# Gated decode attention: keys and values of an item loaded together, x and gate as rows, the normaliser in the PSUM copy

## The chip, the cores and the metric

The kernel runs on one core of a Trainium2 chip. The metric is device time in microseconds (us) of one launch. Five engines run their own instruction lists: TensorE (PE, matmuls), VectorE (DVE), ScalarE (ACT), GpSimd (POOL) and SyncE (SP). Loads are issued by SP and ACT into DMA queues that 16 DMA engines work off.

## The reference

Two decode tokens (B = 2) attend over a cache of 4096 keys and values in 32 heads of 128; beside it stands a small feed-forward network, and a gate mixes both. All is float32.

```python
g = sigmoid((x * gate_w).sum(-1, keepdims=True))            # x: (2, 1, 640)
q = (x @ wq).reshape(B, 1, 32, 128).transpose(0, 2, 1, 3)
p = softmax(einsum("bhqd,bhkd->bhqk", q, k_cache) * 128**-0.5)
a = einsum("bhqk,bhkd->bhqd", p, v_cache).transpose(0, 2, 1, 3).reshape(B, 1, 4096) @ wo
b = silu(x @ w1) @ w2                                       # w1: (640, 1728)
out = g * a + (1 - g) * b
```

Keys and values are 134 MB each, so nearly all of the 298 MB read are cache.

## The kernel before

The 64 pairs of token and head are cut into 16 items: item i is one group of four heads (hq) for one token (b), the two tokens of a group one after the other. The keys of an item fill one slab of 128 partitions x 16384 floats (8.39 MB): 32 partitions a head, 128 keys on each. The values fill another. All large loads go through one pool of three slabs ("slots"), SLOTS = 3.

What is loaded when is a list written by hand, `stream`: first the query weights `wq` 0 and `wq` 1 (the second with w1), then key and value slabs, in the middle a slab `mid` (w2 and two groups of wo), at the end a slab `end` (six groups of wo). `pump` issues the next loads on SP in the order of the list, each as soon as the load three places earlier is spent; `spend` is called behind the last instruction that reads a slab. SP waits in order, so a load that has to wait holds back those behind it. The order of the instructions on each engine is that of the code (a manual schedule).

For an item, `scores` multiplies the key slab in place by the query (POOL takes the columns from CV on, VectorE the first CV = 88 of 128), VectorE sums over the head dimension, and the key slab is spent. `peak` finds the maximum of each 32 partitions, `weights` takes the exponentials on ACT with the sums beside them, `total` adds the sums with a matmul, `values` multiplies the weights with the value slab (32 matmuls into `pv`) and spends it, `combine` copies `pv` out of PSUM on ACT and picks the wanted blocks with four matmuls, and `scale` multiplies by the gate and the inverse of the total on VectorE. `permute` turns an output group with 16 small matmuls, and `project` multiplies it with wo into the accumulator `acc`, as `ffn_out` does with w2.

Ahead of the items stand `gates` (the sigmoid of the gate), `query_rows` (x @ wq), `query` (one group's query spread over the partitions) and `ffn_in` (x @ w1 and silu). x comes as `xs`, 128 partitions of 2 x 5 floats, and the gate as `gs`, 128 x 5, in runs of 20 bytes on ACT's queue. x is padded to 32 columns in `xz`, the stationary operand of all these matmuls.

Of the kernel before, what the change touches and what calls it, by code (L numbers as in the profile page):

```python
# [15 lines left out]
def tile_gated_decode(  # L16
# [66 lines left out]
    def load_wo(grp, t):  # L83
        at = WO_AT[grp][1]
        nc.sync.dma_start(  # L85
            t[:, at : at + Q * D],
            wo[grp * QD : (grp + 1) * QD, :].rearrange("(p n) d -> p (n d)", n=Q),
        )
# [62 lines left out]
    pz, rs = [], []  # L151
    for i in range(2):
        t = const.tile([P, NG, 32], F32, name=f"pz{i}")
        nc.gpsimd.memset(t, 0.0)
# [1 line left out]
        t = const.tile([P, Q], F32, name=f"rs{i}")
        nc.gpsimd.memset(t, 0.0)
        rs.append(t)
    o_first = const.tile([P, Q, 32], F32, name="o_first")
    nc.gpsimd.memset(o_first, 0.0)  # L160

    nc.vector.tensor_copy(xz[:, :, :B], xs.rearrange("p b j -> p j b"))  # L162
# [4 lines left out]
    def gates():
        gx = const.tile([P, B, J], F32, name="gx")
        nc.vector.tensor_mul(gx, xs, gs[:, None, :].to_broadcast([P, B, J]))  # L169
# [32 lines left out]
    def ffn_in():  # L202
        w = T["wq", 1][:, W1_AT : W1_AT + J * F].rearrange("p (j f) -> p j f", j=J)
        rows = ps_s.tile([P, 512], F32, tag="sm", name="hr")
        for j in range(J):
            for c in range(Q):
                nc.tensor.matmul(  # L207
                    rows[32 * c : 32 * c + 32, :QF],
                    xz[:, j, :],
                    w[:, j, c * QF : (c + 1) * QF],  # L210
                    start=(j == 0),
                    stop=(j == J - 1),
                )
        hrow = work.tile([P, 512], F32, tag="osb", name="hrow")
        nc.scalar.copy(hrow[:, :QF], rows[:, :QF])
        tail = ps_s.tile([P, 512], F32, tag="sm", name="hr")
        for j in range(J):
            nc.tensor.matmul(
                tail[:32, :FT], xz[:, j, :], w[:, j, FM:F], start=(j == 0), stop=(j == J - 1)
            )  # L220
        nc.scalar.copy(hrow[:32, QF : QF + FT], tail[:32, :FT])
# [1 line left out]
        ph = ps_s.tile([P, 512], F32, tag="sm", name="ph")
        for n in range(FR):
            for c in range(Q):
                q = slice(32 * c, 32 * c + 32)
                nc.tensor.matmul(  # L227
                    ph[q, n * B : (n + 1) * B],
                    hrow[q, n:QF:FR],
                    ident[q, 32 * c : 32 * c + B],  # L230
                    start=True,
                    stop=True,
                )
        nc.tensor.matmul(
            ph[:FT, FR * B : (FR + 1) * B], hrow[:32, QF : QF + FT], ident[:32, :B], start=True, stop=True
        )
        for n0, n1, m in ((0, FR, P), (FR, FR + 1, FT)):
            k = n1 - n0
            src = ph[:m, n0 * B : n1 * B].rearrange("p (n b) -> p n b", b=B)
            e = const.tile([P, k, B], F32, name=f"he{n0}")[:m]  # L240
            nc.scalar.activation(e, src, AF.Exp, scale=-1.0)  # L241
            nc.vector.tensor_scalar_add(e, e, 1.0)  # L242
# [46 lines left out]
    CV = 88  # L289
    S, M, R, PV, PO, O = {}, {}, {}, {}, {}, {}  # L290

    def scores(i):
# [9 lines left out]
        nc.vector.reduce_sum(S[i], k, axis=AX.X)  # L302
        spend("k", i)

    def peak(i):
        m = work.tile([P, 1], F32, name="m")
        nc.vector.reduce_max(m, S[i], axis=AX.X)  # L307
# [1 line left out]
        nc.vector.tensor_scalar_mul(mb, m.to_broadcast([P, 32]), -SCALE)  # L309
# [1 line left out]
        nc.vector.transpose(mt, mb)
# [34 lines left out]
    def combine(i):  # L346
        osb = work.tile([P, 4, DH], F32, tag="osb", name="osb")
        nc.scalar.copy(osb.rearrange("p c d -> p (c d)"), PV[i])  # L348
# [5 lines left out]
        PO[i] = po

    def scale(i):
        hq, b = items[i]
        r = work.tile([P, Q], F32, name="rinv")
        nc.vector.reciprocal(r, R[i][:, :Q])  # L359
        if b == 0:  # L360
            O[hq] = const.tile([P, Q, B], F32, name=f"oT{hq}")
        nc.vector.scalar_tensor_tensor(  # L362
            O[hq][:, :, b], PO[i][:, :Q], g[:, b : b + 1], r, op0=ALU.mult, op1=ALU.mult
        )

    OP = {}

    def permute(grp):  # L370
        pp = ps_s.tile([P, 512], F32, tag="sm", name="pp")
        for n in range(Q):
            for h in range(Q):
                nc.tensor.matmul(
                    pp[32 * h : 32 * h + 32, n * B : (n + 1) * B],
                    ident[:, n : P : Q],
                    O[grp][:, h, :],
                    start=True,
                    stop=True,
                )  # L380
        OP[grp] = o_first if grp == 0 else const.tile([P, Q, B], F32, name=f"oP{grp}")
        nc.scalar.copy(OP[grp][:, :, :B], pp[:, : Q * B].rearrange("p (n b) -> p n b", b=B))

# [20 lines left out]
    for i in range(N + 1):  # L404
        if i < N:
            scores(i)
            peak(i)
# [2 lines left out]
            weights(i)  # L410
        if i >= 1:
            total(i - 1)
            values(i - 1)
            combine(i - 1)
            scale(i - 1)
        if i == MID + 1:
            middle()
        if i > 2 * WO_MID and i % 2 == 0:
            permute(i // 2 - 1)
# [30 lines left out]
```

## Time and profile before

| | us |
|---|---|
| median of 3 runs | 723.04 (719.76 to 723.85) |
| the profiled execution's own time | 720.28 |
| its span | 718.5 |
| VectorE busy | 504.2 |
| PE busy | 225.8 |
| POOL busy | 179.4 |
| ACT busy | 48.7 |

The span is what the profiler sees of one execution; 1.78 us lie around it. A row of the timeline reads: start, duration, engine, line, operation, output<-input, and in brackets the idle time before it and what ended it. A row of a stretch reads: from:to and its length, busy time of PE, PE's weight load, VectorE, ACT and POOL with the number of instructions, the clock granted to PE, the busy share of the DMA engines and GB/s. A matmul in float32 shows as two records.

### The profile page before, as it was taken

The page shows a single profiled execution, that of the slowest core. Times are in us where ns is not written, and L with a number is a line of the kernel's source. Part 1 is how long each engine was busy: PE and PEld are TensorE (multiplying, and loading weights), DVE is VectorE, ACT ScalarE, POOL GpSimd, SP SyncE. Part 2 cuts the span into 40 slices and gives each one's busy share as a digit, 9 for nine tenths or more (in the row PEclk, how much of TensorE's full clock was granted, in tenths as well). Part 3 has the DMA queues.
Part 4 walks back from the last instruction along what each step waited for, and adds up shares of the span by engine and source line. Part 5 has one row for each costly group of instructions (what it writes and reads, how often), then busy time and mean ns, then how long its engine had stood idle before and what let it go on. Part 6 is the DMA issues. An engine that isn't in the chain of part 4 may idle for free.

```text
span 718.5 us, 4776 instructions
## 1 busy us (share of the span) xinstructions
PE 225.8 (31%) x2078; PEld 98.6 (14%) x2078; DVE 504.2 (70%) x153; ACT 48.7 (7%) x168; POOL 179.4 (25%) x28
## 2 busy tenths in 40 slices
PE   0081022141321406065051524225040615041474
PEld 0021000111110202024011121102010211011123
DVE  1007999797969595970786959595959778695920
ACT  0010010101010101010010010101010101001010
POOL 1006601404123150600606041321406060604100
PEclk9996557565565756577565656656575657565589
DMA  9999976899999999999999999999999999999995
GB/s 409 404 426 464 412 293 292 347 413 423 449 412 460 417 449 417 421 433 409 434 435 434 435 423 452 413 441 431 438 431 420 445 431 431 441 424 439 413 414 245
DMA packets 7013, 298.57 MB, mean 416 GB/s; under 512 B 1160, under 2 KB 1168, under 8 KB 1232
## 3 DMA queue, kind: packets, MB, share of 16 engines
q1 hardware_dynamic: 6568, 298.26, 96.6%
q8 instruction: 16, 0.26, 0.1%
q10 hardware_dynamic: 424, 0.01, 0.0%
q14 instruction: 5, 0.04, 0.0%
HBM read 298.26 MB, written 0.01 MB: 415 GB/s over the span
## 4 chain that ended last, share of the span: by engine, by line
DMA 52%; DVE 43%; PE 3%; issue 1%; ACT 0%; SPq 0%; DVEq 0%; ACTq 0%
DMA k<-in_A_k_cache_dram 43%; DVE s L302 24%; DVE k L298 17%; DMA gs<-in_gate_w_dram 5%; DMA end<-in_A_wo_dram 4%; DVE he L242 2%; PE qr L266 1%; DVE mb L309 1%; PE hr L207 1%; DVE m L307 0%; PE ph L227 0%; ACT pz L318 0%; PE po L351 0%; SPq L85 0%; PE acc L191 0%
## 5 line engine op out<-in xcount | busy, mean ns | idle before, releaser
L295 POOL TENSOR_TENSOR k<-k,qsb 128x5120 f32<-128x5120 f32 x16 | 176.5, 11034 | 486.9 <-DMA k<-in_A_k_cache_dram 486.9
L302 DVE TENSOR_REDUCE s<-k 128x128 f32<-128x16384 f32 x16 | 275.5, 17220 | 1.9
L337 PE MATMUL pv<-v,pz 128*32 128x512 f32 x1024 | 146.9, 738 | 300.6 <-DMA v<-in_A_v_cache_dram 300.6
L298 DVE TENSOR_TENSOR k<-k,q 128x11264 f32<-128x11264 f32 x16 | 190.2, 11886 | 62.2 <-DMA k<-in_A_k_cache_dram 62.2
L337 PEld LDWEIGHTS pv<-v,pz 128*32 128x32 f32 x1024 | 38.0, 133 | 396.3 <-issue 261.4
L318 ACT ACTIVATE pz<-s,nb 32x128 f32<-32x128 f32 x64 | 25.5, 398 | 551.1 <-DVE rinv L359 508.2
L362 DVE SCALAR_TENSOR_TENSOR oT<-po,g,rinv 128x4 f32<-128x4 f32 x16 | 3.6, 222 | 77.1 <-PE po L351 77.1
L351 PE MATMUL po<-sel,osb 128*128 128x4 f32 x128 | 27.0, 334 | 96.5 <-ACT osb L348 96.5
L351 PEld LDWEIGHTS po<-sel,osb 128*128 128x128 f32 x128 | 25.6, 296 | 111.0 <-ACT osb L348 111.0
L242 DVE TENSOR_SCALAR he<-he 128x26 f32<-128x26 f32 (+1 forms) x2 | 11.1, 5553 | 17.6 <-ACT he L241 17.6
L329 PE MATMUL tot<-rs,ones 128*128 128x4 f32 x32 | 8.1, 324 | 44.7 <-issue 44.7
L162 DVE COPY xz<-xs 128x10 f32<-128x10 f32 x1 | 0.2, 173 | 24.1 <-DMA xs<-in_A_x_dram 24.1
L329 PEld LDWEIGHTS tot<-rs,ones 128*128 128x128 f32 x32 | 8.4, 321 | 44.9 <-issue 44.9
L173 PE MATMUL gl<-gp,ones 128*128 128x2 f32 x2 | 0.6, 364 | 38.6 <-DVE gp L171 38.6
L318 ACT ACTIVATION_READ_ACCUMULATOR pz<-s,nb 32x1 f32 x64 | 11.8, 184 | 0.0
L266 PE MATMUL qr<-wq,xz 128*32 128x512 f32 x80 | 10.3, 674 | 0.0
L348 ACT COPY osb<-pv 128x512 f32<-128x512 f32 x16 | 9.4, 585 | 11.3 <-PE pv L337 11.0
L424 DVE COPY ot<-acc 128x160 f32<-128x160 f32 x1 | 0.3, 325 | 13.2 <-PE acc L191 13.2
L191 PE MATMUL acc<-end,oP 128*2 128x160 f32 x192 | 7.4, 299 | 5.1 <-DMA end<-in_A_wo_dram 5.1
L283 PE MATMUL q<-qrow,spread 128*128 128x128 f32 x32 | 8.2, 400 | 0.0
L169 DVE TENSOR_TENSOR gx<-xs,gs 128x10 f32<-128x10 f32 x1 | 0.2, 170 | 10.1 <-DMA gs<-in_gate_w_dram 10.1
L309 DVE TENSOR_SCALAR mb<-m 128x32 f32<-128x32 f32 x16 | 6.6, 410 | 0.6
(53 smaller groups left out, 80.3 us busy)
## 6 DMA issues: line engine op xcount, KB each, us to landing
v<-in_A_v_cache_dram SPq DMA_DIRECT2D x2, 4096.0 KB
end<-in_A_wo_dram SPq DMA_DIRECT2D x6, 1280.0 KB, 19.3
wq<-in_B_w_dram SPq DMA_DIRECT2D x1, 4320.0 KB, 36.7
mid<-in_B_w_dram SPq DMA_DIRECT2D x1, 4160.0 KB, 44.3
mid<-in_A_wo_dram SPq DMA_DIRECT2D x2, 1280.0 KB, 32.7
wq<-in_A_wq_dram SPq DMA_DIRECT2D x1, 2048.0 KB, 26.8
k<-in_A_k_cache_dram SPq DMA_DIRECT2D x16, 47.6
v<-in_A_v_cache_dram SPq DMA_DIRECT2D x15, 28.7
```

The costliest lines, as they stand in the source:

```text
L242: nc.vector.tensor_scalar_add(e, e, 1.0)
L266: nc.tensor.matmul(ps[u][32 * q : 32 * q + 32, :], xz[:, j, :], w[:, u * half : (u + 1) * half, q, :], start=(j == 0), stop=(j == J - 1),)
L283: nc.tensor.matmul(qps[hq][:, b, :], spread[:, b, :], qrow[:, hq, :], start=True, stop=True)
L295: nc.gpsimd.tensor_mul(k[:, CV:, :], k[:, CV:, :], qsb[hq][:, b, None, :].to_broadcast([P, C - CV, DH]))
L298: nc.vector.tensor_mul(k[:, :CV, :], k[:, :CV, :], qps[hq][:, b, None, :].to_broadcast([P, CV, DH]))
L302: nc.vector.reduce_sum(S[i], k, axis=AX.X)
L309: nc.vector.tensor_scalar_mul(mb, m.to_broadcast([P, 32]), -SCALE)
L318: nc.scalar.activation(pz[i % 2][lo:hi, :, 4 * q : 4 * q + 4], S[i][lo:hi].rearrange("p (g c) -> p g c", c=4), AF.Exp, bias=M[i][lo:hi], s ...
L329: nc.tensor.matmul(t[:, :Q], ones, rs[i % 2], start=True, stop=True)
L337: nc.tensor.matmul(PV[i][32 * q : 32 * q + 32, :], pz[i % 2][:, gr, :], v[:, gr, :], start=(gr < 4), stop=(gr >= NG - 4),)
L348: nc.scalar.copy(osb.rearrange("p c d -> p (c d)"), PV[i])
L351: nc.tensor.matmul(po[:, :Q], osb[:, c, :], sel[:, c : 4 * Q : 4], start=(c == 0), stop=(c == 3))
```

## The change

- **Order of the loads.** Up to item 5 keys and values of an item follow each other (k0, v0, k1, v1, ...), then come k6, `mid`, k7, v6, k8, v7 and so on. Before, the keys stood one item ahead throughout. The last group of wo is loaded in two pieces.
- **x and gate as rows.** They are loaded as two and one rows of 640 floats into spare columns of the second `wq` slab, and five matmuls turn them in `gates`.
- **ffn_in.** The rows of x @ w1 are turned by VectorE transposes straight from PSUM in place of 53 small matmuls and two ACT copies; the tail's matmuls stand among the others.
- **The scores.** CV goes from 88 to 68. `products` (the multiplies) and `scores` (the sums) are apart, the sum in two parts at CV, with `total`, `invert`, `values` and `combine` of the item before between them. The intermediate values of `peak` are in PSUM.
- **The normaliser.** The sums are one column, `total` adds the four heads apart with the matrix `fold`, `invert` makes the inverse times the gate, and the copy out of PSUM in `combine` multiplies by it. The four matmuls of `combine` write rows of 128 columns, for both tokens into one PSUM tile (`orow`), with `pick` as the stationary operand; `turn` transposes that on VectorE in place of `permute`.
- **Buffers.** One query buffer in PSUM and one in SBUF instead of two each.

```diff
-    stream = [("wq", 0), ("wq", 1), ("k", 0)]
+    stream = [("wq", 0), ("wq", 1)]
     for i in range(N):
-        if i + 1 < N:
-            stream.append(("k", i + 1))
-        stream.append(("v", i))
-        if i == MID:
-            stream.append(("mid", 0))
-    stream.append(("end", 0))
+        if i <= MID:
+            stream += [("k", i), ("v", i)]
+        elif i == MID + 1:
+            stream += [("k", i), ("mid", 0)]
+        else:
+            stream += [("k", i), ("v", i - 1)]
+    stream += [("v", N - 1), ("end", 0)]
...
-    xs = const.tile([P, B, J], F32, name="xs")
-    nc.scalar.dma_start(xs, x.rearrange("b s (p j) -> p (b s) j", j=J))
-    gs = const.tile([P, J], F32, name="gs")
-    nc.scalar.dma_start(gs, gate.rearrange("(p j) -> p j", j=J))
+    xg = T["wq", 1][: B + 1, XG_AT : XG_AT + D]
+    nc.scalar.dma_start(xg[:B], x.rearrange("b s d -> (b s) d"))
+    nc.scalar.dma_start(xg[B : B + 1], gate[None, :])
...
+        xT = ps_s.tile([P, 512], F32, tag="sm", name="xT")
+        for j in range(J):
+            nc.tensor.matmul(
+                xT[:, j * (B + 1) : (j + 1) * (B + 1)],
+                xg[:, j:D:J],
+                ident[: B + 1, : B + 1],
...
+        for src, m, k, dst in ((rows, P, FR, hT), (tail, FT, 1, hTt)):
+            turned = work.tile([P, 512], F32, tag="osb", name="turned")
+            turned = turned[:m, : 32 * k].rearrange("p (n r) -> p n r", r=32)
+            nc.vector.transpose(turned, src[:m, : 32 * k].rearrange("p (i n) -> p n i", n=k))
...
-    CV = 88
+    CV = 68
...
-        nc.vector.reduce_sum(S[i], k, axis=AX.X)
+        for c0, c1 in ((0, CV), (CV, C)):
+            nc.vector.reduce_sum(S[i][:, c0:c1], k[:, c0:c1, :], axis=AX.X)
         spend("k", i)
...
-        mb = work.tile([P, 32], F32, name="mb")
-        nc.vector.tensor_scalar_mul(mb, m.to_broadcast([P, 32]), -SCALE)
+        nc.vector.tensor_scalar_mul(t[:, 32:64], t[:, :1].to_broadcast([P, 32]), -SCALE)
...
+    def invert(i):
+        t = R[i]
+        nc.vector.reciprocal(t[:, 1:2], t[:, :1])
+        b = items[i][1]
+        R[i] = work.tile([P, 1], F32, name="rg")
+        nc.vector.tensor_scalar(R[i], t[:, 1:2], g[:, b : b + 1], None, op0=ALU.mult)
...
-        nc.scalar.copy(osb.rearrange("p c d -> p (c d)"), PV[i])
+        nc.scalar.activation(osb.rearrange("p c d -> p (c d)"), PV[i], AF.Copy, scale=R[i])
...
+    def turn(hq):
+        OP[hq] = const.tile([P, Q, 32], F32, name=f"oP{hq}")
+        nc.vector.transpose(OP[hq], PO[hq].rearrange("p (i n) -> p n i", n=Q))
...
     for i in range(N + 1):
         if i < N:
+            products(i)
+        if i >= 1:
+            total(i - 1)
+            invert(i - 1)
+            values(i - 1)
+            combine(i - 1)
+        if i == MID + 1:
+            middle()
+        if i < N:
             scores(i)
             peak(i)
+            weights(i)
             if i + 1 < N and items[i + 1][1] == 0:
                 query(items[i + 1][0])
...
```

SP's loads at the start, before, with the engines and DMA counters each one waits for (a wait for PE or DVE is the wait for a slab to be spent):

```order
L101 DMA wq<-in_A_wq_dram 128x16384
L103 DMA wq<-in_A_wq_dram 128x4096
L104 DMA wq<-in_B_w_dram 128x8640
L97 DMA k<-in_A_k_cache_dram 128x16384
L97 DMA k<-in_A_k_cache_dram 128x16384 [waits DMAHW1_49,PE_49]
L97 DMA v<-in_A_v_cache_dram 128x16384 [waits DMAHW4_49,DMAHW3_49,PE_49]
L97 DMA k<-in_A_k_cache_dram 128x16384 [waits DMAHW5_49,DMAHW0_49,DVE_49]
L97 DMA v<-in_A_v_cache_dram 128x16384 [waits DMAHW6_49,DVE_49]
L97 DMA k<-in_A_k_cache_dram 128x16384 [waits DMAHW7_49,DMAHW2_49,PE_49]
```

And with the change:

```order
L104 DMA wq<-in_A_wq_dram 128x16384
L106 DMA wq<-in_A_wq_dram 128x4096
L107 DMA wq<-in_B_w_dram 128x8640
L100 DMA k<-in_A_k_cache_dram 128x16384
L100 DMA v<-in_A_v_cache_dram 128x16384 [waits DMAHW0_49,PE_49]
L100 DMA k<-in_A_k_cache_dram 128x16384 [waits DMAHW3_49,DMAHW2_49,DMAHW4_49,DMAHW1_49,PE_49]
L100 DMA v<-in_A_v_cache_dram 128x16384 [waits DMAHW5_49,DVE_49]
L100 DMA k<-in_A_k_cache_dram 128x16384 [waits DMAHW6_49,PE_49]
L100 DMA v<-in_A_v_cache_dram 128x16384 [waits DMAHW7_49,DVE_49]
```

The sixth load was v0 and is now k1; the seventh waits for VectorE (k0 spent) in both, but it was k2 and is now v1, and k2 stands behind it.

VectorE around items 0 and 1 before, from the tail of the ffn rows to the second reduction:

```order
L242 TENSOR_SCALAR he_279<-he_279 64x2 [waits Activation_49]
L243 RECIPROCAL he_279<-he_279 64x2 [waits DVE_49]
L244 TENSOR_TENSOR he_279<-he_279,gc 64x2 [waits DVE_49]
L245 TENSOR_TENSOR hT<-ph,he_279 64x2 [waits DVE_49]
L298 TENSOR_TENSOR k<-k,q 128x11264 [waits DMAHW5_49]
L302 TENSOR_REDUCE s<-k 128x128 [waits DVE_49,Pool_49]
L307 TENSOR_REDUCE m<-s 128x1 [waits DVE_49]
L309 TENSOR_SCALAR mb<-m 128x32 [waits DVE_49]
L311 STREAM_TRANSPOSE mt<-mb 128x32 [waits DVE_49]
L313 TENSOR_REDUCE nb<-mt 128x1 [waits DVE_49]
L298 TENSOR_TENSOR k<-k,q 128x11264 [waits DMAHW6_49,DMAHW1_49]
L302 TENSOR_REDUCE s<-k 128x128 [waits DVE_49,Pool_49]
```

And with the change, item 0's multiply to item 1's second reduction:

```order
L304 TENSOR_TENSOR k<-k,q 128x8704 [waits DMAHW5_49]
L312 TENSOR_REDUCE s<-k 128x68 [waits DVE_49]
L312 TENSOR_REDUCE s<-k 128x60 [waits Pool_49]
L317 TENSOR_REDUCE m<-s 128x1 [waits DVE_49]
L318 TENSOR_SCALAR m<-m 128x32 [waits DVE_49]
L319 STREAM_TRANSPOSE m<-m 128x32 [waits DVE_49]
L321 TENSOR_REDUCE nb<-m 128x1 [waits DVE_49]
L304 TENSOR_TENSOR k<-k,q 128x8704 [waits DMAHW4_49,DMAHW3_49,DMAHW7_49,DMAHW2_49,DMAHW1_49]
L343 RECIPROCAL tot<-tot 128x1 [waits PE_49]
L346 TENSOR_SCALAR rg<-tot,g 128x1 [waits DVE_49]
L312 TENSOR_REDUCE s<-k 128x68
L312 TENSOR_REDUCE s<-k 128x60 [waits Pool_49]
```

Only the second reduction waits for POOL now, and the two operations of `invert`, which wait for PE, stand between the multiply and the reductions.

PE at the start, before:

```order
L173 MATMUL gl<-gp,ones 128x2 [waits DVE_49]
L266 MATMUL qr<-wq,xz 32x512 [waits DMAHW1_49,Pool_49]
L266 MATMUL qr<-wq,xz 32x512 x31
L266 MATMUL qr<-wq,xz 32x512 [waits DMAHW3_49]
L266 MATMUL qr<-wq,xz 32x512 x7
```

And with the change:

```order
L175 MATMUL xT<-ident,wq 128x3 [waits DMAHW2_49,DMAHW1_49,Pool_49]
L175 MATMUL xT<-ident,wq 128x3 x4
L190 MATMUL gl<-gp,ones 128x2 [waits DVE_49]
L272 MATMUL qr<-wq,xz 32x512 [waits DMAHW0_49,Pool_49]
L272 MATMUL qr<-wq,xz 32x512 x3
```

The five matmuls that turn x and gate stand first and wait for the two row loads (counters 2 and 1) and the identity from POOL; the first wait for a weight slab (counter 0, `wq` 0) is behind them.

More of the change, by code (lines that the diff above doesn't have):

```diff
@@ L51, in tile_gated_decode @@
     work = ctx.enter_context(tc.tile_pool(name="work", bufs=2))
-    ps_q = ctx.enter_context(tc.tile_pool(name="ps_q", bufs=2, space=bass.MemoryType.PSUM))
+    ps_q = ctx.enter_context(tc.tile_pool(name="ps_q", bufs=1, space=bass.MemoryType.PSUM))
+    ps_r = ctx.enter_context(tc.tile_pool(name="ps_r", bufs=1, space=bass.MemoryType.PSUM))
     ps_pv = ctx.enter_context(tc.tile_pool(name="ps_pv", bufs=2, space=bass.MemoryType.PSUM))
@@ L64, in tile_gated_decode @@
     W1_AT = (J - J0) * H * DH
+    XG_AT = W1_AT + J * F
     W2T_AT = FR * D
@@ L84, in load_wo @@
         at = WO_AT[grp][1]
[L85 to L88, printed above, removed]
+        src = wo[grp * QD : (grp + 1) * QD, :].rearrange("(p n) d -> p (n d)", n=Q)
+        cuts = (0, Q * D - D, Q * D) if grp == HQ - 1 else (0, Q * D)
+        for c0, c1 in zip(cuts, cuts[1:]):
+            nc.sync.dma_start(t[:, at + c0 : at + c1], src[:, c0:c1])
     def load(what, n, t):
@@ L139, in tile_gated_decode @@
     nc.vector.memset(ones, 1.0)
+    fold = const.tile([P, 2 * Q, Q, 4], F32, name="fold")
+    nc.vector.memset(fold, 0.0)
+    for q in range(Q):
+        nc.vector.memset(fold[q * QP : (q + 1) * QP, :, q, :], 1.0)
     sel = const.tile([P, 4 * Q], F32, name="sel")
     nc.vector.reduce_sum(sel, ident.rearrange("p (a b) -> p b a", b=32)[:, : 4 * Q, :], axis=AX.X)
+    pick = const.tile([P, 4, P + 1], F32, name="pick")
+    nc.vector.memset(pick, 0.0)
+    for c in range(4):
+        nc.vector.tensor_copy(pick[:, c, 1 : P + 1 : 32], sel[:, c : 4 * Q : 4])
     spread = const.tile([P, B, P], F32, name="spread")
@@ L155, in tile_gated_decode @@
         pz.append(t)
[L156 to L162, printed above, removed]
     g = const.tile([P, B], F32, name="g")
     gc = const.tile([P, B], F32, name="gc")
-    hT = const.tile([P, FR + 1, B], F32, name="hT")
+    hT = const.tile([P, FR, B], F32, name="hT")
+    hTt = const.tile([FT, 1, B], F32, name="hTt")
     def gates():
+        xT = ps_s.tile([P, 512], F32, tag="sm", name="xT")
[4 more added lines that the diff above has]
+                ident[: B + 1, : B + 1],
+                start=True,
+                stop=True,
+            )
+        xT = xT[:, : J * (B + 1)].rearrange("p (j r) -> p j r", j=J)
+        nc.vector.tensor_copy(xz[:, :, :B], xT[:, :, :B])
         gx = const.tile([P, B, J], F32, name="gx")
-        nc.vector.tensor_mul(gx, xs, gs[:, None, :].to_broadcast([P, B, J]))
+        for b in range(B):
+            nc.vector.tensor_mul(gx[:, b, :], xT[:, :, B], xz[:, :, b])
         gp = const.tile([P, B], F32, name="gp")
@@ L204, in ffn_in @@
         rows = ps_s.tile([P, 512], F32, tag="sm", name="hr")
+        tail = ps_s.tile([P, 512], F32, tag="sm", name="hr")
         for j in range(J):
@@ L213, in ffn_in @@
                 )
[L214 to L221, printed above, removed]
-        spend("wq", 1)
[L223 to L241, printed above, removed]
+            for c in range(FT // 32):
+                nc.tensor.matmul(
+                    tail[32 * c : 32 * c + 32, :32],
+                    xz[:, j, :],
+                    w[:, j, FM + 32 * c : FM + 32 * c + 32],
+                    start=(j == 0),
+                    stop=(j == J - 1),
+                )
+        spend("wq", 1)
+        for src, m, k, dst in ((rows, P, FR, hT), (tail, FT, 1, hTt)):
+            turned = work.tile([P, 512], F32, tag="osb", name="turned")
+            turned = turned[:m, : 32 * k].rearrange("p (n r) -> p n r", r=32)
+            nc.vector.transpose(turned, src[:m, : 32 * k].rearrange("p (i n) -> p n i", n=k))
+            h = turned[:, :, :B]
+            e = const.tile([P, k, B], F32, name=f"he{k}")[:m]
+            nc.scalar.activation(e, h, AF.Exp, scale=-1.0)
             nc.vector.tensor_scalar_add(e, e, 1.0)
@@ L283, in query, with products @@
             nc.tensor.matmul(qps[hq][:, b, :], spread[:, b, :], qrow[:, hq, :], start=True, stop=True)
-        qsb[hq] = work.tile([P, B, DH], F32, name="qsb")
+        qsb[hq] = work.tile([P, B, DH], F32, name="qsb", bufs=1)
         nc.scalar.copy(qsb[hq], qps[hq])
-    CV = 88
-    S, M, R, PV, PO, O = {}, {}, {}, {}, {}, {}
-    def scores(i):
+    CV = 68
+    S, M, R, PV, PO, OP = {}, {}, {}, {}, {}, {}
+    def products(i):
         hq, b = items[i]
@@ L328, in total @@
         t = ps_s.tile([P, 512], F32, tag="sm", name="tot")
-        nc.tensor.matmul(t[:, :Q], ones, rs[i % 2], start=True, stop=True)
+        nc.tensor.matmul(t[:, :1], fold.rearrange("p a q c -> p (a q c)"), R[i], start=True, stop=True)
         R[i] = t
+    def invert(i):
[4 more added lines that the diff above has]
+        nc.vector.tensor_scalar(R[i], t[:, 1:2], g[:, b : b + 1], None, op0=ALU.mult)
     def values(i):
@@ L346, in combine @@
     def combine(i):
+        hq, b = items[i]
         osb = work.tile([P, 4, DH], F32, tag="osb", name="osb")
-        nc.scalar.copy(osb.rearrange("p c d -> p (c d)"), PV[i])
-        po = ps_s.tile([P, 512], F32, tag="sm", name="po")
+        nc.scalar.activation(osb.rearrange("p c d -> p (c d)"), PV[i], AF.Copy, scale=R[i])
+        if b == 0:
+            PO[hq] = ps_r.tile([P, DH], F32, name="orow")
         for c in range(4):
             nc.tensor.matmul(
-                po[:, :Q], osb[:, c, :], sel[:, c : 4 * Q : 4], start=(c == 0), stop=(c == 3)
-            )
[L354 to L382, printed above, removed]
+                PO[hq],
+                pick[:, c, 1 - b : P + 1 - b],
+                osb[:, c, :],
+                start=(b == 0 and c == 0),
+                stop=(b == B - 1 and c == 3),
+            )
+    def turn(hq):
+        OP[hq] = const.tile([P, Q, 32], F32, name=f"oP{hq}")
+        nc.vector.transpose(OP[hq], PO[hq].rearrange("p (i n) -> p n i", n=Q))
     def project(grp):
@@ L390, in middle @@
     def middle():
-        for grp in range(WO_MID):
-            permute(grp)
         for grp in range(WO_MID):
@@ L405, in tile_gated_decode @@
         if i < N:
+            products(i)
[7 more added lines that the diff above has]
+        if i < N:
             scores(i)
             peak(i)
+            weights(i)
             if i + 1 < N and items[i + 1][1] == 0:
                 query(items[i + 1][0])
[L410 to L419, printed above, removed]
+        if i >= 1 and items[i - 1][1] == B - 1:
+            turn(items[i - 1][0])
     for grp in range(WO_MID, HQ):
```

22 lines of the change are left out of this document (12 added, 10 removed).

## The prediction

> **What bounds the kernel now.** I read the slices of the page first, then the chain, the busy time by stretches, SP's issues in time, and last the rows around each hole. First the page (40 slices of 18 us each), the chain's shares and the bytes:
>
> ```profile
> DMA  9999976899999999999999999999999999999995
> GB/s 409 404 426 464 412 293 292 347 413 423 449 412 460 417 449 417 421 433 409 434 435 434 435 423 452 413 441 431 438 431 420 445 431 431 441 424 439 413 414 245
> HBM read 298.26 MB, written 0.01 MB: 415 GB/s over the span
> DMA 52%; DVE 43%; PE 3%; issue 1%; ACT 0%; SPq 0%; DVEq 0%; ACTq 0%
> ```
>
> The DMA engines are full except in slices 5 to 7 and the last. So the loads set the end, although the chain gives VectorE (DVE) 43%: there it follows VectorE's freeing of slots while the next load was queued already. The stretches show the holes (last column GB/s, before it the DMA share):
>
> ```profile
> 0.00:58.60 58.60, 18.57 (x246) 8.13 (x246) 4.53 (x20) 4.01 (x9) 2.87 (x12) 1.00 0.98 416
> 58.60:95.00 36.40, 0.00 (x0) 0.00 (x0) 36.12 (x6) 0.05 (x1) 21.97 (x2) 0.51 1.00 432
> 95.00:100.00 5.00, 0.00 (x0) 0.00 (x0) 4.90 (x4) 0.00 (x0) 0.00 (x0) 0.50 0.00 0
> 95.00:145.00 50.00, 11.82 (x76) 4.90 (x76) 45.01 (x14) 4.87 (x18) 10.98 (x1) 0.60 0.70 294
> 145.00:320.00 175.00, 56.44 (x368) 22.83 (x368) 145.06 (x39) 12.36 (x44) 44.20 (x4) 0.62 1.00 432
> 320.00:690.00 370.00, 120.36 (x1088) 53.38 (x1088) 272.58 (x72) 26.65 (x96) 99.39 (x9) 0.62 1.00 431
> 690.00:713.00 23.00, 17.36 (x270) 8.62 (x270) 0.63 (x3) 0.75 (x2) 0.00 (x0) 0.91 0.90 376
> ```
>
> A full queue moves 431 to 432 GB/s; I take 431.5. Against that the stretches lose 58.6 x (1 - 416/431.5) = 2.1 us at the start, 50 x (1 - 294/431.5) = 15.9 us in 95:145, 5.0 of them in the empty 95:100, and 3.0 us at the end. The 15.9 us are two holes with their ramps, of 5.0 and 10.9. SP's issues and waits say why:
>
> ```profile
> 2.10 45.97 SPq L97 DMA_DIRECT2D k<-in_A_k_cache_dram  x2
> 54.23 0.33 SPq L97 DMA_DIRECT2D v<-in_A_v_cache_dram  x1
> 99.32 0.33 SPq L97 DMA_DIRECT2D k<-in_A_k_cache_dram  x1
> 129.44 0.33 SPq L97 DMA_DIRECT2D v<-in_A_v_cache_dram  x1
> SPq L97 <- DMA wq<-in_A_wq_dram: 20.0, 1, 20.0
> SPq L97 <- PE qr L266: 24.9, 1, 24.9
> wq<-in_B_w_dram SPq DMA_DIRECT2D x1, 4320.0 KB, 36.7
> ```
>
> SP waits 20.0 us for the first slab of wq (landed at about 2.6 + 20.0 = 22.6), then 24.9 us for the query matmuls that free it: k1 goes out at 47.6, v0 at 54.2. Both were queued behind k0, so at 8.39 MB each and 38.9 us for the two they end near 97. k2 must wait until k0 is spent (99.32), v1 until k1 is spent (129.44): these are the holes. Why k0 is spent so late:
>
> ```profile
> 27.92 0.17 DVE L162 COPY xz<-xs 128x10 f32<-128x10 f32 x1 [24.10 <-DMA xs<-in_A_x_dram]
> 38.18 0.17 DVE L169 TENSOR_TENSOR gx<-xs,gs 128x10 f32<-128x10 f32 x1 [10.09 <-DMA gs<-in_gate_w_dram]
> 39.12 10.28 PE L266 MATMUL qr<-wq,xz 128*32 128x512 f32 x80
> 49.97 3.70 PE L207 MATMUL hr<-wq,xz 128*32 128x416 f32 x40
> 58.63 10.96 POOL L295 TENSOR_TENSOR k<-k,qsb 128x5120 f32<-128x5120 f32 x1 [55.16 <-DMA k<-in_A_k_cache_dram]
> 58.68 10.93 DVE L242 TENSOR_SCALAR he<-he 64x2 f32<-64x2 f32 x1 [0.23 <-ACT he L241]
> 70.09 11.87 DVE L298 TENSOR_TENSOR k<-k,q 128x11264 f32<-128x11264 f32 x1
> 78.01 11.01 POOL L295 TENSOR_TENSOR k<-k,qsb 128x5120 f32<-128x5120 f32 x1 [8.42 <-DMA k<-in_A_k_cache_dram]
> 82.07 17.22 DVE L302 TENSOR_REDUCE s<-k 128x128 f32<-128x16384 f32 x1
> 129.76 3.85 DVE L309 TENSOR_SCALAR mb<-m 128x32 f32<-128x32 f32 x1
> ```
>
> The small loads of x and gate land at 27.9 and 38.2, and TensorE (PE) stands still until then, 16 us after wq. k0 lands at 58.6, but VectorE is held 10.93 us in a 64x2 operation, exactly as long as GpSimd's (POOL) multiply, and starts on k0 at 70.09. The same kind of operation (L309) took 3.85 us at 129.76.
>
> **The change part by part.** *Order of the loads.* Now wq0, wq1, k0, v0, k1, v1 up to item 5, then k6, mid, k7, v6 as before. Three slots: v0 takes wq0's, k1 takes wq1's, v1 takes k0's, k2 takes v0's. *x and gate as rows:* two loads of two and one rows instead of 384 runs of 20 bytes. Bounds of landing: at once, or 38.2 as now. I take about 6 us: the 27.2 us of xs were 16 rows per engine and a closing write, 1.6 us each, and about four such turns are left. The Trainium skill, "DMA: Bandwidth & Descriptors", Queues, rings and completion order, says that an engine goes round the queue rows packet by packet; that gives the same four turns, and the rows of xs agree. The query matmuls then begin when wq0 lands, at 22.6. Their first 64 records take 8.2 us (10.28 x 64/80): v0 goes out at 31. The ffn rows begin when w1 has landed (36.7 us after an issue just before 2.1: 38.5) and take 3.7 us plus at most 1.4 for the ten small tail matmuls: k1 goes out at 43.6. Both are there before k0 lands at 58.6, so v0 lands at 78.0 and k1 at 97.5. Even x at 38.2 would leave both in time (47.6 and 54.2).
>
> *Work on one item.* Durations of before, and a settled stretch:
>
> ```profile
> L295 POOL TENSOR_TENSOR k<-k,qsb 128x5120 f32<-128x5120 f32 x16 | 176.5, 11034 | 486.9 <-DMA k<-in_A_k_cache_dram 486.9
> L302 DVE TENSOR_REDUCE s<-k 128x128 f32<-128x16384 f32 x16 | 275.5, 17220 | 1.9
> L298 DVE TENSOR_TENSOR k<-k,q 128x11264 f32<-128x11264 f32 x16 | 190.2, 11886 | 62.2 <-DMA k<-in_A_k_cache_dram 62.2
> L311 DVE STREAM_TRANSPOSE mt<-mb 128x32 f32<-128x32 f32 x16 | 3.4, 212 | 0.6
> 288.20 11.89 DVE L298 TENSOR_TENSOR k<-k,q 128x11264 f32<-128x11264 f32 x1 [3.54 <-DMA k<-in_A_k_cache_dram]
> 317.44 0.29 DVE L307 TENSOR_REDUCE m<-s 128x1 f32<-128x128 f32 x1
> 320.57 0.58 ACT L348 COPY osb<-pv 128x512 f32<-128x512 f32 x1
> 307.64 9.12 PE L337 MATMUL pv<-v,pz 128*32 128x512 f32 x64 [22.81 <-DMA v<-in_A_v_cache_dram]
> 323.25 2.36 PE L191 MATMUL acc<-mid,o_first 128*32 128x160 f32 x32
> 333.97 0.66 PE L374 MATMUL pp<-oT,ident 128*32 128x2 f32 x32
> ```
>
> CV goes from 88 to 68. VectorE multiplies 11.89 x 68/88 = 9.2 us, does the two new normaliser operations (0.4), reduces its 68 columns in 9.15 and the other 60 in 8.07. GpSimd multiplies 11.03 x 60/40 = 16.55 us, done before the second reduction begins at 18.7. A key slab is spent 27 us after landing, against 29.2 (317.44 - 288.20). An item's loads take 38.9 us. v(i) needs k(i-1) spent, 27 us after that landed, and its turn in the queue comes at 38.9: 12 us to spare. k(i) needs v(i-2) spent: the peak and the weights take 3.1 (317.44 to 320.57) and the values 9.1, so 40 us after k(i-2) landed, where its turn comes at 58: 18 us. Around mid (7.05 MB, 16.3 us): k7 waits for v5, 14 us to spare; v6 for k6, 27 against 16.3 + 19.4 = 35.7, 8.7 us, the smallest; k8 for mid, whose matmuls took 10.7 us (323.25 to 333.97), 28 us. So no hole is left: -15.9 us.
>
> *New waits.* invert stands on VectorE between the multiply and the reductions, and waits for the total on PE, which stands behind the combine two items back; both are done some 32 us after the key before landed, 7 us before the next, so the reductions behind it don't wait. On ScalarE (ACT) the weights stand behind the PSUM copy of the item before, which in the later items waits for its values: 19.4 + 9.1 + 0.6 = 29 us after the key, when the weights would begin anyway. With one query buffer instead of two the next query follows that combine on PE, near 32, before the next key at 38.9. Each of these would have to be late by more than 8.7 us to open a hole.
>
> *First key.* With the ffn over by 46, nothing of VectorE's stands beside GpSimd's first multiply: k0 is spent at 58.6 + 27 = 86 instead of 99.3, before the queue runs dry at 97.5. If the 10.9 us came back, it would be 97: still in time.
>
> *Work that moves at no cost.* Transposes of ffn rows: up to 13 blocks x 0.21 = 2.8 us, between 43 and 58.6. Eight output transposes of up to 4 x 0.21 = 0.85 us, behind combine, about 32 us after a key's landing, 6 us before the next. Four 128-column matmuls in combine instead of four of 4 columns, both under 2 us; the permuting matmuls (0.66 us a group) go. All this is covered by waits for loads, and would cost its own duration, under 1 us an item, if that cover went. The set-up of fold and pick, some 2 us on VectorE, hides under the wait for wq0. Fewer small packets at the start: between 0 and 2.1 us; first bytes can't come sooner, I take 0.3.
>
> *The end.* The last 1.28 MB piece of wo comes in two:
>
> ```profile
> 713.59 1.27 PE L191 MATMUL acc<-end,oP 128*2 128x160 f32 x32 [1.91 <-DMA end<-in_A_wo_dram]
> 714.93 0.33 DVE L424 COPY ot<-acc 128x160 f32<-128x160 f32 x1 [13.20 <-PE acc L191]
> ```
>
> 32 records behind the last landing become 8, and three quarters of the work comes 0.8 us earlier: -0.8, between 0 and -1.0.
>
> **Sum.** 718.5 - 15.9 - 0.3 - 0.8 = 701.5 us of span. The profiled execution took 720.28, 1.78 beyond its span: 703.3. The median of the runs is 723.04, 2.76 above it, which would make it 706.0. I say 704.5, between the two.
>
> **Rivals.** (B) *A new wait in the place of the old.* Keys are no longer loaded one item ahead in the first six items, so a late slot opens a hole at once. A hole as the first or second now would leave 5.0 to 10.9 us: 709.5 to 715.4. For it: GpSimd's multiply becomes half as long again, and its 16.55 us are only scaled. Against it: at least 8.7 us to spare everywhere.
>
> (C) *The loads slow down and nothing is won.* At 421.5 GB/s the same bytes take 16 us more: 720.5. For it: single slices of the page stand at 409 to 420, and the first stretch at 416. Against it: two long stretches with the same transfers at 431 and 432. The Trainium skill, "SBUF — State Buffer", SBUF: two separate sides, puts HBM to one core at about 358 GB/s; the bytes would then take an estimated 833 us, and the 415 GB/s of this span contradict it.
>
> (D) *Slower: GpSimd's longer multiply locks VectorE out.* The rows at 58.68 and 129.76 show operations that end with GpSimd's. If VectorE's multiply also had to wait, an item would take 16.55 + 9.2 + 17.2 = 43 us against 38.9: 4.1 x 16 = 66 us more, on top of 704.5: about 770. Slower than before begins where an item takes over 38.9 + 1 us, 16 items eating the 17 won. Against it: L298 at 288.20 runs 11.89 us beside GpSimd, L302 at 82.07 its usual 17.22. The Trainium skill, "SBUF — State Buffer", Who interferes with whom, says that a reduction never contends here and that an operation with one SBUF input outside the two-port modes doesn't; the new normaliser operations read PSUM, as does the multiply. By the same section a scaling from SBUF to SBUF does block, as L242 did. If the normaliser step blocked all the same, the key would be spent at 34, still before 38.9.
>
> **How the numbers follow.** Forecast 0.82; B 0.09; C 0.06; D 0.03. Faster by over 0.5% (about what a measurement of this kernel can tell): 0.82 + 0.09 = 0.91; C gives no change, 0.06; D slower, 0.03. The range goes from 700.5 (the profiled execution's sum with the whole 2.1 us of the start and 1.0 at the end) to 710.5 (the median's sum with a hole of 4.5 us).
>
> **What would show it.** Right: SP issues v0 near 31 and k1 near 44; DMA slices at 9 throughout except the last; VectorE starts on k0 near 58.7 and GpSimd's multiply takes 16.5 us; the last landing is near 697. Wrong: a zero in the DMA row between 90 and 320; xT waiting for the load of x beyond 22; a second reduction waiting for GpSimd; or the full stretches below 428 GB/s.

## The result, and the profile after

The changed kernel takes 703.64 us (median of four runs, 702.96 to 703.98) against 723.33 (719.76 to 723.85): a ratio of 0.9737, 95% interval 0.9705 to 0.9769. The forecast was 704.5, in a range of 700.5 to 710.5. The profiled execution took 702.96, with a span of 701.2; the working had 703.3 and 701.5. In one experiment below (the scaling in GpSimd's way) the profiled execution was a disturbed one of 716.94 us: only the duration of an instruction is read from it, and the time given is that of the other three.

The page of the kernel after, its slices of DMA share and GB/s:

```profile
DMA  9999999999999999999999999999999999999996
GB/s 419 399 449 422 434 457 419 422 430 453 422 426 426 460 420 426 421 413 426 445 416 445 430 441 416 449 426 437 423 437 430 435 434 434 427 438 437 409 415 259
HBM read 298.26 MB, written 0.01 MB: 425 GB/s over the span
```

The 7, 6 and 8 in slices 5 to 7 (counted from 0) are gone. By stretches (last two columns: DMA share, GB/s):

```profile
0.00:58.60 58.60, 19.52 (x156) 8.21 (x156) 6.04 (x38) 3.42 (x7) 2.66 (x10) 0.86 0.98 419
95.00:145.00 50.00, 15.74 (x110) 6.01 (x102) 36.55 (x10) 3.02 (x10) 25.36 (x2) 0.69 1.00 432
145.00:320.00 175.00, 59.94 (x488) 26.36 (x488) 129.90 (x48) 13.18 (x44) 73.50 (x5) 0.62 1.00 429
320.00:690.00 370.00, 114.00 (x852) 40.94 (x852) 250.66 (x88) 25.72 (x90) 148.08 (x9) 0.64 1.00 431
```

95:145 moves 432 GB/s instead of 294: 50 x (432 - 294) / 431.5 = 16.0 us of transfer are back. The other stretches shown move within 3 GB/s of what they moved before. Why, in SP's issues and the first rows of PE, VectorE and GpSimd (start, duration):

```profile
31.37 0.33 SPq L100 DMA_DIRECT2D v<-in_A_v_cache_dram  x1
44.97 0.33 SPq L100 DMA_DIRECT2D k<-in_A_k_cache_dram  x1
85.04 0.33 SPq L100 DMA_DIRECT2D v<-in_A_v_cache_dram  x1
98.45 0.33 SPq L100 DMA_DIRECT2D k<-in_A_k_cache_dram  x1
10.31 2.33 PE L175 MATMUL xT<-ident,wq 3*128 3x3 f32 x10 [10.31 <-DMA wq<-in_gate_w_dram]
22.84 10.19 PE L272 MATMUL qr<-wq,xz 128*32 128x512 f32 x80 [8.81 <-DMA wq<-in_A_wq_dram]
47.76 0.15 DVE L251 TENSOR_TENSOR hTt<-turned,he 64x2 f32<-64x2 f32 x1
58.47 9.22 DVE L304 TENSOR_TENSOR k<-k,q 128x8704 f32<-128x8704 f32 x1 [10.56 <-DMA k<-in_A_k_cache_dram]
58.59 16.45 POOL L301 TENSOR_TENSOR k<-k,qsb 128x7680 f32<-128x7680 f32 x1 [55.34 <-DMA k<-in_A_k_cache_dram]
67.73 17.28 DVE L312 TENSOR_REDUCE s<-k 128x68 f32<-128x8704 f32 x2
97.30 9.22 DVE L304 TENSOR_TENSOR k<-k,q 128x8704 f32<-128x8704 f32 x1 [11.23 <-DMA k<-in_A_k_cache_dram]
```

x and gate are there at 10.3, the query matmuls begin with the first slab of wq at 22.84 (39.12 before), the ffn is over at 47.9, VectorE begins k0 when it lands (58.47 against 70.09) and spends it at 85.04 (99.32 before). VectorE now waits some 11 us for these keys: it has become the engine with time to spare.

### The profile page after: what moved, and what is told of

Same layout as the page of the kernel before. It is cut to its first block, busy times and chain, and to the rows that moved or that the text cites. A ratio compares the mean times of both kernels' runs of the same rounds, so it can differ in the third digit from the quotient of the medians.

```text
span 701.2 us, 4091 instructions
## 1 busy us (share of the span) xinstructions
PE 219.8 (31%) x1736; PEld 85.8 (12%) x1736; DVE 450.8 (64%) x190; ACT 47.3 (7%) x158; POOL 266.0 (38%) x25
## 4 chain that ended last, share of the span: by engine, by line
DMA 59%; DVE 27%; PE 9%; another core or an unknown queue 2%; ACT 1%; issue 0%; SPq 0%; DVEq 0%; ACTq 0%
DMA k<-in_A_k_cache_dram 37%; DVE s L312 17%; DMA v<-in_A_v_cache_dram 13%; DVE k L304 9%; PE pv L353 8%; DMA wq<-in_B_w_dram 5%; DMA end<-in_A_wo_dram 4%; ACT pz L327 1%; PE hr L225 1%; PE tot L338 0%; SPq L91 0%; DVE rg L346 0%; PE acc L208 0%; DVE m L317 0%
## 5 line engine op out<-in xcount | busy, mean ns | idle before, releaser
L301 POOL TENSOR_TENSOR k<-k,qsb 128x7680 f32<-128x7680 f32 x16 | 263.4, 16462 | 389.2 <-DMA k<-in_A_k_cache_dram 389.2
L312 DVE TENSOR_REDUCE s<-k 128x68 f32<-128x8704 f32 (+1 forms) x32 | 276.3, 8677 | 0.0
L304 DVE TENSOR_TENSOR k<-k,q 128x8704 f32<-128x8704 f32 x16 | 147.5, 9221 | 160.7 <-DMA k<-in_A_k_cache_dram 160.7
L338 PE MATMUL tot<-rs,fold 128*128 128x1 f32 x32 | 7.5, 305 | 141.5 <-ACT pz L327 141.5
L369 PE MATMUL orow<-osb,pick 128*128 128x128 f32 x128 | 24.0, 345 | 64.1 <-ACT osb L365 64.1
L365 ACT ACTIVATE osb<-pv,rg 128x512 f32<-128x512 f32 x16 | 11.0, 687 | 448.1 <-PE pv L353 337.9
L369 PEld LDWEIGHTS orow<-osb,pick 128*128 128x128 f32 x128 | 20.4, 242 | 78.6 <-ACT osb L365 78.6
L338 PEld LDWEIGHTS tot<-rs,fold 128*128 128x128 f32 x32 | 6.2, 241 | 145.2 <-ACT pz L327 145.2
L225 PE MATMUL hr<-wq,xz 128*32 128x416 f32 x40 | 5.7, 706 | 5.5 <-DMA wq<-in_B_w_dram 5.5
L289 PEld LDWEIGHTS q<-qrow,spread 128*128 128x128 f32 x32 | 5.5, 245 | 0.8 <-ACT qrow L282 0.8
L175 PE MATMUL xT<-ident,wq 3*128 3x3 f32 x10 | 2.3, 355 | 10.3 <-DMA wq<-in_gate_w_dram 10.3
```

The costliest lines, as they stand in the source:

```text
L225: nc.tensor.matmul(rows[32 * c : 32 * c + 32, :QF], xz[:, j, :], w[:, j, c * QF : (c + 1) * QF], start=(j == 0), stop=(j == J - 1),)
L289: nc.tensor.matmul(qps[hq][:, b, :], spread[:, b, :], qrow[:, hq, :], start=True, stop=True)
L301: nc.gpsimd.tensor_mul(k[:, CV:, :], k[:, CV:, :], qsb[hq][:, b, None, :].to_broadcast([P, C - CV, DH]))
L304: nc.vector.tensor_mul(k[:, :CV, :], k[:, :CV, :], qps[hq][:, b, None, :].to_broadcast([P, CV, DH]))
L312: nc.vector.reduce_sum(S[i][:, c0:c1], k[:, c0:c1, :], axis=AX.X)
L338: nc.tensor.matmul(t[:, :1], fold.rearrange("p a q c -> p (a q c)"), R[i], start=True, stop=True)
```

## The experiments

Theory 1: before the change the loads stopped because the first key slab was spent late (99.3) with a queue that ran dry at 97, and the next ones late in turn; what ends this is any part that frees the slabs in time. Theory 2: the order of the loads ends it. Theory 3: x and gate as rows end it. Ratios are to the kernel before, run on the same chip.

**The old order of loads in the changed kernel** (`stream` as before, everything else as in the changed kernel).

> The changed kernel with the old order of loads (keys one item ahead throughout). Theory 1 (late freeing: the holes of before came because the first key slab was spent at 99 us, after the queue ran dry at 97, and the second at 129): here the first key starts at 58.5 and is spent at 85, k1 is spent near 113 before k2 has landed at 117, so no hole opens: 703.6 us, within 0.5% of the changed kernel. Theory 2 (the order of the loads is what removes the holes): they come back, 15.9 us: about 719.5. Theory 3 (only the late x was at fault): 703.6.

Measured: 705.18 us (704.44 to 705.5), ratio 0.9759 (0.9724 to 0.9793), which can't be told from the changed kernel's 0.9737. The times themselves are 1.5 us apart, but they come from two sets of runs; whether the order is worth that much stays open. Its profile shows k2's load on time and then v1's and k3's:

```profile
85.17 0.33 SPq L99 DMA_DIRECT2D k<-in_A_k_cache_dram  x1
112.87 0.33 SPq L99 DMA_DIRECT2D v<-in_A_v_cache_dram  x1
113.29 0.39 SPq L99 DMA_DIRECT2D k<-in_A_k_cache_dram  x1
```

112.87 is 4 us ahead of k2's landing (VectorE starts on it at 116.75). Theory 2 falls: with the other parts there, the order isn't needed.

**The new order alone**, in the kernel before.

> The kernel before with the new order of loads alone. Theory 1: VectorE still starts on k0 near 70 and spends it at 99, so v1 comes 2 us after the queue is dry plus a ramp of some 2 us, a hole of 3.5 to 5; k1 has landed at 97, so the peak's scaling of item 0 is held by GpSimd to about 108 and k2 may come 2 us late as well: 4 to 7 us lost of the 15.9, 708 to 712 us. Theory 2: all of the gain, 704.5. Theory 3: none of it, 720 to 723.

Measured: 712.56 us (711.43 to 713.64) against 721.56, ratio 0.9857 (0.9814 to 0.99). This is a part of the gain, 9.0 us; the time is half a microsecond above the slowest that theory 1 allowed. The rows of its profile show both of the losses that it named:

```profile
58.88 10.87 DVE L243 TENSOR_SCALAR he<-he 64x2 f32<-64x2 f32 x1 [0.23 <-ACT he L242]
99.46 0.33 SPq L98 DMA_DIRECT2D v<-in_A_v_cache_dram  x1
99.79 8.71 DVE L310 TENSOR_SCALAR mb<-m 128x32 f32<-128x32 f32 x1
120.75 0.33 SPq L98 DMA_DIRECT2D k<-in_A_k_cache_dram  x1
```

The ffn's 64x2 scaling is held for 10.87 us, so v1 is issued at 99.46, after the queue is dry; the peak's scaling is held for 8.71 us by GpSimd's multiply of k1, so the weights, the values and with them k2 come late too.

**x and gate as rows alone**, in the kernel before (the two loads, the five turning matmuls, nothing else).

> The kernel before with x and gate loaded as rows, and nothing else. Theory 1: the ffn is over by 48 us, k0 is begun at 58.6 and spent at 88, and a hole of 3 to 5 us is left before v1 near 118, since k1 needs 29.2 us on VectorE and k2 has landed at 117. Because k2 has then landed before the peak of item 1, its scaling from SBUF to SBUF is held by GpSimd's 11 us multiply, which makes the next key late in turn; if that goes on through items 1 to 5 the loss is up to 33 us. 708 us without this chain, up to 736 with it; I expect 715 to 736. Theory 2: 720 to 723. Theory 3: 704.5.

Measured: 738.3 us (738.08 to 738.9), ratio 1.022 (1.0184 to 1.0255): slower than before by 16.7 us, 2 us beyond the upper end of what theory 1 gave. The DMA slices of its page, the peak's scaling at items 0 to 2 and over all items, and a wait behind it at item 1:

```profile
DMA  9999997989979897995999999999999999999995
88.67 0.96 DVE L320 TENSOR_SCALAR mb<-m 128x32 f32<-128x32 f32 x1
119.58 8.72 DVE L320 TENSOR_SCALAR mb<-m 128x32 f32<-128x32 f32 x1
163.15 9.49 DVE L320 TENSOR_SCALAR mb<-m 128x32 f32<-128x32 f32 x1
L320 DVE TENSOR_SCALAR mb<-m 128x32 f32<-128x32 f32 x16 | 47.8, 2989 | 0.6
133.46 0.22 DVE L373 SCALAR_TENSOR_TENSOR oT<-po,g,rinv 128x4 f32<-128x4 f32 x1 [4.61 <-PE po L362]
```

k0 is spent at 88, as reckoned, and still the loads stop again and again up to slice 18. An operation of 0.18 us is held at each of the items 1 to 5, for 8.56 to 9.65 us, because GpSimd already multiplies the next key when the peak of this one comes; the next key is then begun late, and its peak meets GpSimd again. From k1's spending (119.25) to k2's (162.82) an item takes 43.6 us, against 38.9 for its loads. Of the 43.6 us 8.7 are the hold, and 4.61 are VectorE's wait for PE in `scale`, which the change replaces by `invert`. Without the hold the item takes 35.1 us, as the kernel with the peak in PSUM shows below; without the wait it would, by subtraction, take 39.0. Theory 3 falls: the part that starts everything sooner is a loss by itself.

**The scalings in PSUM alone**, in the kernel before: the exponentials of the ffn rows and the peak's small tiles go to PSUM.

```diff
...
-            nc.scalar.activation(e, src, AF.Exp, scale=-1.0)
-            nc.vector.tensor_scalar_add(e, e, 1.0)
-            nc.vector.reciprocal(e, e)
+            nc.scalar.activation(ep, src, AF.Exp, scale=-1.0)
+            nc.vector.tensor_scalar_add(ep, ep, 1.0)
+            nc.vector.reciprocal(ep, ep)
...
-        nc.vector.tensor_scalar_mul(mb, m.to_broadcast([P, 32]), -SCALE)
+        nc.vector.tensor_scalar_mul(t[:, 32:64], t[:, :1].to_broadcast([P, 32]), -SCALE)
```

> The kernel before with the scalings of the ffn rows and of the peak working in PSUM instead of from SBUF to SBUF, so that GpSimd's multiply doesn't hold them; x is late and the order of loads is old. Theory 1: the 10.9 us of the 64x2 operation go to 0.2, k0 is begun at 59.5 and spent at 89, before the queue is dry at 97; k1 is spent at 118.5 against k2's landing at 117, a hole of 3.5 to 6 us with its ramp is left: 10 to 12 us gained, 708 to 713 us. Theory 2 and theory 3: 720 to 723.

Measured: 710.57 us (709.46 to 711.99), ratio 0.9836 (0.9799 to 0.9873), 11.0 us gained. In its profile the same scaling takes 0.16 us beside GpSimd, and k2 and v1 are issued at:

```profile
58.91 0.16 DVE L243 TENSOR_SCALAR hp<-hp 64x2 f32<-64x2 f32 x1 [0.27 <-ACT hp L242]
88.79 0.33 SPq L97 DMA_DIRECT2D k<-in_A_k_cache_dram  x1
118.96 0.33 SPq L97 DMA_DIRECT2D v<-in_A_v_cache_dram  x1
```

Moving these two small tiles out of GpSimd's way gains about as much as the new order: 11.0 us against 9.0, with runs that overlap (709.46 to 711.99 and 711.43 to 713.64). The 64x2 tile alone was not moved. In the kernel with x as rows alone its scaling was out of GpSimd's way too, and the peak's was held all the same. What is left here is the hole before v1, since k2 has landed by 117.

**The peak in SBUF again, in the changed kernel**, with the new order and with the old one.

> The changed kernel with the small tiles of the peak in SBUF again, as before the change. Theory 1: with the new order of loads the next key lands 38.9 us after the last, when the peak (27 us) is long over, so GpSimd isn't running and nothing is held: 703.6 us. Rival (the SBUF scaling is held at every item): 16 x up to 16.5 us of VectorE time, 740 us or more.

> The changed kernel with the old order of loads and the peak in SBUF: x early and ffn early, but neither protection against GpSimd. Theory 1: k1 has landed at 78 and GpSimd works on it from 78 to 94.5, so the scaling of item 0 at 85.4 is held for 9 us, k1 is spent near 122 against k2's landing at 117, and the scaling of item 1 is held too: 8 to 35 us lost, 711 to 738 us. Rival (the place of the peak's tiles doesn't matter): 705, as the old order alone.

Measured: 703.14 us (702.99 to 704.35), ratio 0.9731 (0.9699 to 0.9762), with the new order; 712.38 us (712.18 to 712.57), ratio 0.9859 (0.9833 to 0.9886), with the old one. The peak's scaling in the one profile and in the other:

```profile
L319 DVE TENSOR_SCALAR mb<-m 128x32 f32<-128x32 f32 x16 | 2.9, 182 | 0.6
```

```profile
L318 DVE TENSOR_SCALAR mb<-m 128x32 f32<-128x32 f32 x16 | 11.7, 734 | 0.6
85.29 9.03 DVE L318 TENSOR_SCALAR mb<-m 128x32 f32<-128x32 f32 x1
121.46 0.33 SPq L99 DMA_DIRECT2D v<-in_A_v_cache_dram  x1
```

With the new order it is held nowhere; with the old one once, at item 0, for 9.03 us. That makes k1 late (121.46 against 112.87) and costs 712.38 - 705.18 = 7.2 us; the chain of the kernel with x as rows alone doesn't form here. From k0's spending to k1's the item takes 121.46 - 84.96 = 36.5 us with the hold in it, still less than the 38.9 us of its loads. Either protection is enough, the order or PSUM; without both the gain is halved.

**6.05 us more work on each key** before it is spent (the first 45 columns summed once more), with the new order and with the old one.

```diff
...
+        nc.vector.reduce_sum(spare, k[:, :45, :], axis=AX.X)
         spend("k", i)
```

> The changed kernel with 6.05 us more of VectorE work on each item before the key slab is spent (the first 45 columns are summed once more, into a spare tile). Theory 1: the key is spent 32.6 us after landing instead of 26.6; the smallest room, at mid, was put at 8.7 us and the usual one at 12, so no hole opens: 703.6 us, within 0.5% of the changed kernel. Rival (the rooms are smaller than said, or each microsecond on an item counts): up to 16 x 6 = 97 us more.

> The same 6.05 us an item, with the old order of loads. Theory 1: here k1 is already there when k0 is spent, so the early items run back to back on VectorE and each delay adds to the one before: k0 spent at 91, k1 at 125 against k2's landing at 117, k2 some 34 us after that against k3's: holes of about 11 us in all with their ramps, 714 to 717 us. That is what the new order of loads is worth once the rest is there: nothing as it stands, some 11 us when items are slower. Rival (the order makes no difference): 703.6 like the kernel with the new order.

Measured: 702.73 us (702.5 to 703.62), ratio 0.9728 (0.9701 to 0.9755), and 711.66 us (711.52 to 712.14), ratio 0.9851 (0.9824 to 0.9877). With the new order 97 us of added VectorE work cost nothing. With the old one a hole opens, at item 2 alone, and the time is 2.3 us below the expected range. In that kernel v1 came into v0's slab and k3 into k1's, so v1 was not late; k2's multiply begins at 128.00, behind a wait for the query's copy, and the next two loads are issued at 160.87 and 161.29, when the last one had landed at 155.37:

```profile
128.00 9.22 DVE L304 TENSOR_TENSOR k<-k,q 128x8704 f32<-128x8704 f32 x1 [2.52 <-ACT qsb L291]
155.37 16.45 POOL L301 TENSOR_TENSOR k<-k,qsb 128x7680 f32<-128x7680 f32 x1 [10.78 <-DMA k<-in_A_k_cache_dram]
160.87 0.33 SPq L99 DMA_DIRECT2D v<-in_A_v_cache_dram  x1
```

So the order of the loads is room, not time: worth nothing that can be told as the kernel stands, and 8.9 us when items are 6 us slower.

**14 us more work on each key** (104 columns), new order.

> The changed kernel with 14.0 us more VectorE work on each item before the key slab is spent (104 columns summed once more). Theory 1: an item then takes 40.6 us to spend its key and 1.2 us for the peak behind it, 41.8 against the 38.9 us of its loads, so VectorE sets the pace from the second item on: 15 x 2.9 = 44 us more and a few us of ramps, 745 to 760 us. Rival (some other slack hides it): 704 to 720.

Measured: 768.07 us (767.44 to 768.3), ratio 1.0631 (1.0606 to 1.0657), 8 us beyond the expected range. VectorE sets the pace, as said, but every second item waits once more:

```profile
99.68 9.22 DVE L305 TENSOR_TENSOR k<-k,q 128x8704 f32<-128x8704 f32 x1
143.80 9.22 DVE L305 TENSOR_TENSOR k<-k,q 128x8704 f32<-128x8704 f32 x1 [2.52 <-ACT qsb L292]
185.55 9.18 DVE L305 TENSOR_TENSOR k<-k,q 128x8704 f32<-128x8704 f32 x1
```

Two items take 185.55 - 99.68 = 85.9 us, 42.9 each; (42.9 - 38.9) x 16 = 64 us, and 703.6 + 64 = 767.6. The 2.52 us are the wait for the next group's query, which the expectation left out: ACT copies it at 143.40, right behind the weights of the last item, where the changed code puts it (before, `query` stood ahead of `weights`). No run puts it back. In the changed kernel this lies in the time in which VectorE waits for the key.

**A scaling from SBUF to SBUF in GpSimd's way** at each item of the changed kernel.

```diff
...
+        nc.vector.tensor_scalar_mul(two, one, 2.0)
         R[i] = work.tile([P, 1], F32, name="rg")
```

> The changed kernel with one more 128x32 scaling from SBUF to SBUF on VectorE between the multiply and the reductions of each item, while GpSimd's 16.5 us multiply runs. Theory 1 (such a scaling is held until GpSimd is done, but there is room for it): the scaling takes about 7 us instead of 0.2, the key is spent 34 us after landing instead of 26.6, the room of 8.7 to 12 us takes it: 703.6 us. Rival (the prediction's slower case: it costs what it takes): 15 x 7 = 105 us more, about 808. Rival 2 (nothing is held there): the scaling takes 0.2 us.

Measured: 704.95 us (703.91 to 704.97), ratio 0.9752 (0.9727 to 0.9776). The duration of the new scaling, mean of 16 (busy us, mean ns):

```profile
L348 DVE TENSOR_SCALAR two<-one 128x32 f32<-128x32 f32 x16 | 110.6, 6912 | 0.0
```

It takes 7.3 us (median) at 15 items and 0.17 at the last, beside which GpSimd doesn't run, 110.6 us in all; the time's median is 1.3 us above the changed kernel's, which its spread doesn't tell from nothing. This is the prediction's slower rival in its milder form: the lock is real, and the room takes it.

**CV = 88 again**, and **the last wo in one piece**, each in the changed kernel.

> The changed kernel with CV = 88 again, GpSimd taking 40 columns instead of 60. Theory 1: the key is spent 29.2 us after landing instead of 26.6, inside the room: 703.6 us, within 0.5%. Rival (the new share of the columns brings part of the gain): 2.6 us for each of 16 items, up to 42 us more.

> The changed kernel with the last 1.28 MB of wo loaded in one piece. The prediction's term: 24 more records of matmuls stand behind the last landing, 0.8 us (0 to 1.0): 704.4 us, and the time from the start of the last group's matmuls to the copy of the result stays 1.3 us while the wait ahead of it grows by about 0.7. Rival (the end is set by the output's write alone): no change in the span beyond 0.1 us.

Measured: 704.28 us (703.56 to 704.34), ratio 0.9745 (0.9725 to 0.9765), and 704.2 us (703.52 to 704.79), ratio 0.9746 (0.9725 to 0.9767). Neither can be told from the changed kernel by its time. The end of the second one's profile, and then that of the changed kernel:

```profile
693.72 1.27 PE L208 MATMUL acc<-end,oP 128*2 128x160 f32 x32 [1.82 <-DMA end<-in_A_wo_dram]
696.90 1.27 PE L208 MATMUL acc<-end,oP 128*2 128x160 f32 x32 [1.92 <-DMA end<-in_A_wo_dram]
698.23 0.33 DVE L423 COPY ot<-acc 128x160 f32<-128x160 f32 x1 [11.12 <-PE acc L208]
```

```profile
693.65 1.27 PE L208 MATMUL acc<-end,oP 128*2 128x160 f32 x32 [1.83 <-DMA end<-in_A_wo_dram]
696.09 1.27 PE L208 MATMUL acc<-end,oP 128*2 128x160 f32 x32 [1.16 <-DMA end<-in_A_wo_dram]
697.42 0.33 DVE L423 COPY ot<-acc 128x160 f32<-128x160 f32 x1 [11.79 <-PE acc L208]
```

From one group's matmuls to the next 3.18 us with one piece and 2.44 with two: the cut is worth 0.74 us.

Not tried: the late x inside the changed kernel; the rows of x together with the peak in PSUM in the kernel before; and by themselves the normaliser in the PSUM copy, the sums in two parts or the transposes.

## Why the prediction was right, point by point

- *The holes, 15.9 us.* Right: 16.0 by the stretch 95:145. The settled rate held (429 to 432 GB/s), so the loads didn't slow down, rival C.
- *The start, 0.3 us.* 58.6 x (419 - 416) / 431.5 = 0.4. *The end, 0.8 us.* 0.74. Sum: 17.0 expected, 718.5 - 701.2 = 17.3 found.
- *The times on the way.* v0 at 31 (31.37), k1 at 43.6 (44.97; the ffn's matmuls took 5.8 us instead of 5.1), k0 spent at 86 (85.04), GpSimd's multiply 16.55 us (16.45). x and gate were taken to land at 6 and came at 10.3; the wait for wq to 22.84 covers both.
- *The room.* 12 us and 8.7 at mid: 6 us more cost nothing; with 14 us more an item takes longer than its loads, and it cost 64. So the room lies between the two.
- *The lock, rival D.* The reasons against it held: the multiply takes 9.22 us beside GpSimd, the two reductions 17.28 together. Where the lock was put in on purpose, it cost what the prediction said of the normaliser step: nothing.
- *The range.* Its lower end doesn't follow from the terms named for it: 718.5 - 15.9 - 2.1 - 1.0 + 1.78 = 701.3, not 700.5. The measured 703.64 lies inside either way.
- *What it didn't see.* The sum books the 15.9 us under the order of the loads and has the first key as a safeguard. The runs show parts that replace one another: of the three, the order alone gives 9.0 us, the PSUM scalings alone 11.0, the rows alone lose 16.7, and taking the order or the PSUM peak back out of the whole changes nothing that can be told. The size was right because all were there, so its mechanism (no slab is freed too late) held, but crediting the order of the loads with it did not; a forecast of the rows alone by the same working would have had the wrong sign, for it left out where the peak's scaling meets GpSimd once keys arrive ahead. Here 0.18 us became 8.7 and 9.5, and with PSUM tiles it stayed at 0.20 or less. The section that the prediction cites (the Trainium skill, "SBUF — State Buffer", Who interferes with whom) covers this case too: a scaling from SBUF to SBUF can contend with GpSimd, and whichever of the two starts first blocks the other for its whole instruction. The traces agree.
